# Linear attention beside a top-8 expert block: where ScalarE copies turned tile 2, which engine makes tile 3's root, and where G of tile 0 stands

## The chip, the core and the metric

One core of a Trainium2 chip. The metric is the device time of one execution in microseconds (us), the median of several runs. TensorE (PE) multiplies matrices, VectorE (DVE), ScalarE (ACT) and GpSimd (POOL) work on vectors, and SyncE (SP) issues most of the DMAs. Each engine runs its own instructions in order and waits for the others by semaphores. PSUM, where PE writes, has eight banks, called 0 to 7 here.

## What is computed

The input is x with 2048 rows of 640. Two blocks are added to it:

```python
xn = _layernorm(x)                        # over the 640 columns
# A: linear attention, 32 heads of 20
q, k, v = split(xn @ wqkv)
phi = lambda t: jnp.where(t > 0, t + 1, jnp.exp(t)) + 1e-6
pq, pk = phi(q), phi(k)
num = pq @ (pk.T @ v)                     # head by head
den = pq @ pk.sum(over rows) + 1e-6
A = (num / den) @ wo
# B: the 8 rows of xn with the largest xn @ w_r go through an expert
B = xn;  B[idx] += (silu(xs @ w_gate) * (xs @ w_up)) @ w_down * sigmoid(r[idx])
out = x + A + B
```

## The kernel before

The rows are cut into 16 tiles of 128 (t = 0 to 15), the columns into five pieces of 128 (`kc`). The order of every engine's instructions is the order in which the calls stand in the file: nothing is rescheduled, and an engine that waits holds back all that stands behind it.

A tile of the first phase passes these steps:

- `stat(t, b)` (L174): VectorE takes the statistics of one half of the row, and after the second half the mean and variance (`mv`).
- `root_act(t)` (L179) or `root_pool(t)` (L184): one over the standard deviation, `rs`. On ScalarE it is two one-column activations, Ln (L181) and Exp (L182); on GpSimd it is an addition (L186) and a power (L187).
- `norm_dve(t)` (L195): VectorE writes the normalised tile `xn` (L196).
- Turning the tile: tiles 0 to 3 by PE, later ones by DMA. `tr_pe(t)` (L212) is five transposes (L215) into banks 7 and 6. `tr_ev(t, V)` (L219) evicts them into `xnT`: ScalarE copies the first three pieces (L221), VectorE the other two (L226). The same two banks serve the next tile.
- `k_half(t, b)` (L233): five matmuls (L237) that give one half of k, 320 columns. Tile 1 uses banks 2 and 3, tile 2 banks 4 and 5, all others banks 0 and 1.
- `k_act(t, halves)` (L246): ScalarE evicts k. Each half takes two activations of 128 x 320, Exp into `ek` (L251) and Relu into `rk` (L252); after half 1 of all tiles but tile 0, a one-column copy takes the router's score (L254). `k_phi(t)` (L257) then makes phi on VectorE (L259).

`router_col` (L151) puts the router's weights into the k weights as one more column, by one transpose and a copy on ScalarE (L153); since tile 0's k comes before that, `router_0` (L155) gets its score by five one-column matmuls (L157), copied from bank 6 at L163.

Of q there are 20 units of 128 x 512. `q_mm(u, bank)` (L271) is five matmuls (L274), `q_act` (L280) two activations (L283, L284). Units 0 and 2 use bank 7, unit 1 bank 0. G is the product of xn and phi of k, summed over all tiles in banks 2 to 6: `g1(t)` (L264) is five matmuls of 512 columns (L266) per tile. Those banks are free for it once the k of tiles 1 and 2 and the router's score of tile 0 have been read.

The order of calls around the change is written out by hand in L389 to L465 of the file. The middle of it:

```python
    root_act(2)
    router_col()
    k_act(0)
    ...
    root_pool(3)
    const_sel8()
    k_half(1, 0)
    tr_pe(2)
    k_half(1, 1)
    tr_ev(2, V)
    router_0()
    k_act(1)
```

Behind it follow `k_half(2, 0)`, `tr_pe(3)`, `k_half(2, 1)`, `tr_ev(3, V)`, `k_act(2)`, both halves of tile 3, `q_mm(0)`, `q_mm(1, 0)`, `g1(0)`, `q_mm(2)` and tile 4 on PE.

Of the kernel before, what the change touches and what calls it, by code (L numbers as in the profile page):

```python
# [8 lines left out]
P = 128  # L9
# [9 lines left out]
HW = 320  # L19
# [10 lines left out]
BF16 = mybir.dt.bfloat16  # L30
# [8 lines left out]
def kernel(  # L39
# [22 lines left out]
    evk = ctx.enter_context(tc.tile_pool(name="evk", bufs=4))  # L62
# [34 lines left out]
    def load_x(a, b):  # L97
        SP.dma_start(x_sb[:, a:b, :], x_v[:, a:b, :])
# [52 lines left out]
    def router_col():  # L151
        PE.transpose(psb[:, 6, 512 : 512 + KC], wr5[:], ident[0:KC, 0:KC])
        A.copy(wk[:, :, D], psb[:, 6, 512 : 512 + KC])  # L153

    def router_0():  # L155
        for kc in range(KC):
            PE.matmul(  # L157
                ps[:, 6, 400:401], lhsT=xnT[:, kc, 0:P], rhs=wk[:, kc, D : D + 1],
                start=(kc == 0), stop=(kc == KC - 1),
            )  # L160
# [13 lines left out]
    def stat(t, b):  # L174
        V.bn_stats(out=stats[:, t, b, :], in_=x_sb[:, t, b * HW : (b + 1) * HW])  # L175
        if b:
            V.bn_aggr(out=mv[:, t, :], in_=stats[:, t, :, :])  # L177

    def root_act(t):  # L179
        sl = slice(t, t + 1)  # L180
        A.activation(lg[:, sl], mv[:, t, 1:2], AF.Ln, bias=eps5[:])  # L181
        A.activation(rs[:, sl], lg[:, sl], AF.Exp, scale=-0.5)  # L182

    def root_pool(t, n=1):  # L184
        sl = slice(t, t + n)
        G.tensor_scalar_add(t2[:, sl], mv[:, sl, 1], EPS_BF16)  # L186
        G.tensor_tensor(out=rs[:, sl], in0=t2[:, sl], in1=mhalf[:, 0:n], op=ALU.pow)  # L187
# [31 lines left out]
    def tr_ev(t, other=A):  # L219
        dst = xnT[:, :, t * P : (t + 1) * P]  # L220
        A.copy(dst[:, 0:3, :], psb[:, 7, 0 : 3 * P].rearrange("p (k f) -> p k f", k=3))  # L221
        src = psb[:, 6, 0 : 2 * P].rearrange("p (k f) -> p k f", k=2)
        if other is A:
            A.copy(dst[:, 3:, :], src)
        else:
            V.tensor_copy(dst[:, 3:, :], src)  # L226

    def tr_dma(t):
        nc.sync.dma_start_transpose(xnT[:, :, t * P : (t + 1) * P], xn[:, t, :])
# [3 lines left out]
    def k_half(t, b):  # L233
        b0 = K_BANK.get(t, 0)
        n = HW + (b if t else 0)
        for kc in range(KC):
            PE.matmul(  # L237
                ps[:, b0 + b, 0:n],
                lhsT=xnT[:, kc, t * P : (t + 1) * P],
                rhs=wk[:, kc, b * HW : b * HW + n],  # L240
                start=(kc == 0), stop=(kc == KC - 1),
            )

    kev = {}

    def k_act(t, halves=(0, 1)):  # L246
        b0 = K_BANK.get(t, 0)
        e = evk.tile([P, 2, HW], BF16, tag="ek", name=f"ek{t}")
        r = evk.tile([P, 2, HW], BF16, tag="rk", name=f"rk{t}")
        for b in halves:  # L250
            A.activation(e[:, b, :], ps[:, b0 + b, 0:HW], AF.Exp)  # L251
            A.activation(r[:, b, :], ps[:, b0 + b, 0:HW], AF.Relu)  # L252
            if b and t:
                A.copy(r_all[:, t : t + 1], ps[:, b0 + 1, HW : HW + 1])  # L254
        kev[t] = e, r

    def k_phi(t):  # L257
        e, r = kev.pop(t)
# [5 lines left out]
    def g1(t):  # L264
        for c in range(5):
            PE.matmul(  # L266
                ps[:, 2 + c, :], lhsT=xn[:, t, c * P : (c + 1) * P], rhs=pk[:, t, 0:512],
                start=(t == 0), stop=(t == T - 1),
            )

    def q_mm(u, bank=7):  # L271
        tb, m = u // KC, u % KC
        for kc in range(KC):
            PE.matmul(  # L274
                ps[:, bank, :], lhsT=wq[:, kc, m * P : (m + 1) * P],
                rhs=xnT[:, kc, tb * 512 : (tb + 1) * 512],
                start=(kc == 0), stop=(kc == KC - 1),
            )

    def q_act(u, bank=7):  # L280
        e = evq.tile([P, 512], BF16, tag="eq", name=f"eq{u}")
        r = evq.tile([P, 512], BF16, tag="rq", name=f"rq{u}")
        A.activation(e[:], ps[:, bank, :], AF.Exp)  # L283
        A.activation(r[:], ps[:, bank, :], AF.Relu)  # L284
        kev["q", u] = e, r
# [76 lines left out]
    def const_sel8():  # L362
        cst["sel8"] = sb("sel8", [P, C], F32)
        G.memset(cst["sel8"][:], 0.0)
        for j in range(4):
            G.affine_select(
                out=cst["sel8"][:], in_=cst["sel8"][:], compare_op=ALU.not_equal, fill=1.0,
                base=-32 * j, pattern=[[-1, C]], channel_multiplier=1,
            )
# [9 lines left out]
    def stats2(t):  # L379
        stat(t, 0)  # L380
        stat(t, 1)
# [22 lines left out]
    tr_ev(1, V)  # L404
    root_act(2)
    router_col()
    k_act(0)
    stat(3, 0)
    norm_dve(2)
    stat(3, 1)  # L410
    root_pool(3)
    const_sel8()
    k_half(1, 0)
    tr_pe(2)
    k_half(1, 1)
    tr_ev(2, V)
    router_0()
    k_act(1)
    stat(4, 0)
    norm_dve(3)  # L420
# [4 lines left out]
    k_half(2, 1)  # L425
    tr_ev(3, V)
    k_act(2)
    stat(5, 0)
    k_phi(0)
# [11 lines left out]
    norm_dve(5)  # L441
    tr_dma(5)
    q_act(0)
    q_mm(1, 0)
    q_act(1, 0)
    k_phi(1)
    norm_dve(6)
    tr_dma(6)
    load_x(10, 16)
    g1(0)  # L450
    stats2(7)
    root_pool(7)
    k_phi(2)
# [472 lines left out]
```

## Time and profile before

| what | us |
|---|---|
| median of 3 runs | 112.06 |
| lowest and highest | 111.9, 112.12 |
| the profiled execution | 111.9 |
| its span, first to last instruction | 110.2 |
| PE busy in the span | 105.5 |
| DVE busy | 83.9 |
| ACT busy | 61.4 |
| POOL busy | 41.3 |

The profiled execution is the one with the lowest time; 1.7 us of it lie outside the span. In a row of the order of time, the first number is the start in us from the span's start, the second the length of the row; x15 means fifteen instructions in one row, and a bracket gives the idle time ahead of it and what ended it. An instruction on ScalarE or VectorE can be issued while the one before it still runs, so rows overlap. The end of a matmul lies some way behind the issue of the next one.

### The profile page before, as it was taken

To read this page: it belongs to the slowest core of one execution; us is meant where nothing else is said; L and a number is where in the kernel's file an instruction comes from. 1 tells how busy PE (TensorE), PEld (TensorE's weight loads), DVE (VectorE), ACT (ScalarE), POOL (GpSimd) and SP (SyncE) were. 2 spreads that over 40 slices of the span, in tenths; PEclk is the share of its full clock that TensorE was granted. 3 is DMA by queue.
4 is the path that set the end of the run, shared out by engine and by line. 5 is a ranking of instruction groups with operands and counts; after the bars stand their busy time and mean duration, and the time that the engine had idled before them with its cause. 6 is when DMAs were issued, how large, how long until landed. Compare 5 with 4: busy or idle time off the path is not lost.

```text
span 110.2 us, 2558 instructions
## 1 busy us (share of the span) xinstructions
PE 105.5 (96%) x926; PEld 61.9 (56%) x926; DVE 83.9 (76%) x186; ACT 61.4 (56%) x158; POOL 41.3 (38%) x89
## 2 busy tenths in 40 slices
PE   5999999999999999999999999999999999999990
PEld 2256645565555555555437879444447766666660
DVE  1798998799999998756739844698599665788880
ACT  1549996797967666655048372588985645000000
POOL 6913564202366648899997330000000410000310
DMA  2999334792678799889999979549939295783333
GB/s 71 333 343 332 112 68 91 177 273 59 182 184 180 175 125 254 188 169 352 230 301 381 363 245 286 156 110 314 348 60 171 20 343 189 194 320 101 110 122 119
DMA packets 28551, 22.46 MB, mean 204 GB/s; under 512 B 11634, under 2 KB 27258, under 8 KB 28538
## 3 DMA queue, kind: packets, MB, share of 16 engines
q1 hardware_dynamic: 23664, 18.44, 62.3%
q10 hardware_dynamic: 4810, 3.85, 11.4%
q8 instruction: 7, 0.11, 0.5%
q14 instruction: 6, 0.05, 0.2%
q0 software_dynamic: 64, 0.01, 0.2%
HBM read 14.79 MB, written 5.43 MB: 183 GB/s over the span
## 4 chain that ended last, share of the span: by engine, by line
PE 89%; ACT 3%; DMA 2%; DVE 2%; issue 1%; ACTq 0%
PE ps L274 20%; PE ps L823 19%; PE ps L237 18%; PE ps L266 16%; PE ps L522 4%; DMA x_sb<-in_A_x_dram 2%; PE ps L658 2%; PE ps L675 2%; PE ps L758 2%; PE ps L849 1%; PE ps L215 1%; PE ps L590 1%; PE ps L687 1%; DVE xn L196 1%; PE ps L768 1%; DVE stats L175 1%
## 5 line engine op out<-in xcount | busy, mean ns | idle before, releaser
L237 PE MATMUL ps<-wk,xnT 128*128 128x320 bf16 (+1 forms) x160 | 24.8, 300 | 0.1
L274 PE MATMUL ps<-xnT,wq 128*128 128x512 bf16 x100 | 23.7, 379 | 0.0
L823 PE MATMUL ps<-late,pqT 128*128 128x320 bf16 x150 | 21.8, 300 | 0.1
L237 PEld LDWEIGHTS <-xnT 128*128 128x128 bf16 x160 | 15.1, 97 | 8.6 <-ACT xnT L221 0.9
L266 PE MATMUL ps<-pk,xn 128*128 128x512 bf16 x80 | 19.6, 379 | 0.0
L251 ACT ACTIVATE ek<-ps 128x320 bf16<-128x320 f32 x32 | 14.8, 461 | 8.1 <-PE ps L237 8.1
L823 PEld LDWEIGHTS <-pqT 128*128 128x128 bf16 x150 | 13.9, 98 | 7.2 <-DVE pqT L631 1.9
L283 ACT ACTIVATE eq<-ps 128x512 bf16<-128x512 f32 x20 | 12.0, 598 | 8.9 <-PE ps L274 8.9
L290 DVE SCALAR_TENSOR_TENSOR pqT<-eq,rq 128x512 bf16<-128x512 bf16 x20 | 14.2, 709 | 3.5 <-ACT rq L284 3.4
L832 DVE TENSOR_TENSOR o<-ps,x_sb 128x640 bf16<-128x640 f32 x15 | 12.3, 823 | 5.4 <-PE ps L823 3.0
L175 DVE BATCH_NORM_STATS2 stats<-x_sb 128x6 f32<-128x320 bf16 x32 | 14.7, 473 | 2.1 <-DMA x_sb<-in_A_x_dram 1.9
L259 DVE SCALAR_TENSOR_TENSOR pk<-ek,rk 128x640 bf16<-128x640 bf16 x16 | 14.0, 874 | 2.4 <-ACT rk L252 2.3
L274 PEld LDWEIGHTS <-wq 128*128 128x128 bf16 x100 | 9.4, 98 | 10.6 <-issue 0.7
L252 ACT ACTIVATE rk<-ps 128x320 bf16<-128x320 f32 x32 | 14.7, 460 | 0.0
L207 POOL TENSOR_SCALAR x_sb<-x_sb,rs,nm 128x640 bf16<-128x640 bf16 x13 | 12.6, 982 | 0.6
L266 PEld LDWEIGHTS <-xn 128*128 128x128 bf16 x80 | 7.6, 98 | 8.1
L284 ACT ACTIVATE rq<-ps 128x512 bf16<-128x512 f32 x20 | 11.9, 593 | 0.0
L186 POOL TENSOR_SCALAR t<-mv 128x1 bf16<-128x1 f32 x12 | 3.8, 318 | 20.3 <-DVE mv L177 20.0
L196 DVE TENSOR_SCALAR xn<-x_sb,mv,rs 128x640 bf16<-128x640 bf16 x16 | 8.2, 515 | 3.3 <-POOL rs L187 2.8
L187 POOL TENSOR_TENSOR rs<-t,mhalf 128x1 f32<-128x1 bf16 x12 | 10.1, 839 | 1.0
L874 POOL DMA_INDIRECT s_dram<-y,idx_i x1 | 1.6, 1595 | 20.9 <-ACT y L870 20.9
L859 ACT CAST o<-ps 128x160 bf16<-128x160 f32 x1 | 0.3, 293 | 13.9 <-PE ps L849 13.9
(128 smaller groups left out, 105.5 us busy)
## 6 DMA issues: line engine op xcount, KB each, us to landing
wg<-in_B_w_gate_dram SPq DMA_DIRECT2D x5, 384.0 KB, 3.4
wu<-in_B_w_up_dram SPq DMA_DIRECT2D x5, 384.0 KB, 9.0
wd<-in_B_w_down_dram SPq DMA_DIRECT2D x4, 480.0 KB, 11.2
spare<-rd SPq DMA_DIRECT2D x3, 640.0 KB, 5.3
rd<-rden ACTq DMA_DIRECT2D x1, 1280.0 KB, 7.3
out_dram<-o SPq DMA_DIRECT2D x8, 160.0 KB, 1.9
out_dram<-o ACTq DMA_DIRECT2D x7, 160.0 KB, 2.8
wo<-in_A_wo_dram SPq DMA_DIRECT2D x2, 500.0 KB, 7.0
```

Of the source, the lines that this page charges most:

```text
L175: V.bn_stats(out=stats[:, t, b, :], in_=x_sb[:, t, b * HW : (b + 1) * HW])
L207: G.tensor_scalar(out=x_sb[:, t, :], in0=x_sb[:, t, :], scalar1=rs1[:, sl], scalar2=nm[:, sl], op0=ALU.mult, op1=ALU.add,)
L237: PE.matmul(ps[:, b0 + b, 0:n], lhsT=xnT[:, kc, t * P : (t + 1) * P], rhs=wk[:, kc, b * HW : b * HW + n], start=(kc == 0), stop=(kc == KC ...
L251: A.activation(e[:, b, :], ps[:, b0 + b, 0:HW], AF.Exp)
L252: A.activation(r[:, b, :], ps[:, b0 + b, 0:HW], AF.Relu)
L259: V.scalar_tensor_tensor(out=pk[:, t, :].rearrange("p (b f) -> p b f", b=2), in0=e[:], scalar=1.0, in1=r[:], op0=ALU.min, op1=ALU.add,)
L266: PE.matmul(ps[:, 2 + c, :], lhsT=xn[:, t, c * P : (c + 1) * P], rhs=pk[:, t, 0:512], start=(t == 0), stop=(t == T - 1),)
L274: PE.matmul(ps[:, bank, :], lhsT=wq[:, kc, m * P : (m + 1) * P], rhs=xnT[:, kc, tb * 512 : (tb + 1) * 512], start=(kc == 0), stop=(kc == K ...
L283: A.activation(e[:], ps[:, bank, :], AF.Exp)
L290: V.scalar_tensor_tensor(out=pqT[:, m, tb * 512 : (tb + 1) * 512], in0=e[:], scalar=1.0, in1=r[:], op0=ALU.min, op1=ALU.add,)
L823: PE.matmul(ps[:, b0 + b, 0:HW], lhsT=pqT[:, kc, t * P : (t + 1) * P], rhs=Ms[:, kc, b * HW : (b + 1) * HW], start=(kc == 0), stop=(kc == ...
L832: V.tensor_tensor(out=o_t[:], in0=ps[:, b0 : b0 + 2, 0:HW], in1=x_sb[:, t, :].rearrange("p (b f) -> p b f", b=2), op=ALU.add,)
```

## The change

Three things change, and nothing is computed differently:

- `k_act(0)` is cut in two. Half 0 of tile 0's k is evicted where all of it was; half 1 comes behind `tr_ev(2, V)`. So ScalarE's copy of turned tile 2 stands between the halves. For this `k_act` now makes its two tiles at the first call and keeps them for the second.
- The root of tile 3 is made by `root_act(3)` on ScalarE, behind that copy and ahead of half 1, where it was `root_pool(3)` on GpSimd.
- `g1(0)` stands ahead of `q_mm(1, 0)`; it stood four calls behind `q_act(1, 0)`.

```diff
     def k_act(t, halves=(0, 1)):
         b0 = K_BANK.get(t, 0)
-        e = evk.tile([P, 2, HW], BF16, tag="ek", name=f"ek{t}")
-        r = evk.tile([P, 2, HW], BF16, tag="rk", name=f"rk{t}")
+        if t not in kev:
+            e = evk.tile([P, 2, HW], BF16, tag="ek", name=f"ek{t}")
+            r = evk.tile([P, 2, HW], BF16, tag="rk", name=f"rk{t}")
+            kev[t] = e, r
+        e, r = kev[t]
         for b in halves:
             A.activation(e[:, b, :], ps[:, b0 + b, 0:HW], AF.Exp)
             A.activation(r[:, b, :], ps[:, b0 + b, 0:HW], AF.Relu)
             if b and t:
                 A.copy(r_all[:, t : t + 1], ps[:, b0 + 1, HW : HW + 1])
-        kev[t] = e, r
...
     root_act(2)
     router_col()
-    k_act(0)
+    k_act(0, (0,))
     stat(3, 0)
     norm_dve(2)
     stat(3, 1)
-    root_pool(3)
     const_sel8()
     k_half(1, 0)
     tr_pe(2)
     k_half(1, 1)
     tr_ev(2, V)
+    root_act(3)
+    k_act(0, (1,))
     router_0()
     k_act(1)
...
     q_act(0)
+    g1(0)
     q_mm(1, 0)
     q_act(1, 0)
     k_phi(1)
     norm_dve(6)
     tr_dma(6)
     load_x(10, 16)
-    g1(0)
```

ScalarE in the first phase, from the second activation of tile 0's half 0 to the copy of turned tile 3. `ek0` and `rk0` are tile 0's, `ek1` and `rk1` tile 1's; the first `xnT` row is the copy of turned tile 2, the last that of tile 3. Before:

```order
L252 ACTIVATE rk0_212<-ps_72 128x320
L251 ACTIVATE ek0_211<-ps_72 128x320
L252 ACTIVATE rk0_212<-ps_72 128x320
L221 COPY xnT_80<-ps_72 128x3x128
L251 ACTIVATE ek1_259<-ps_72 128x320
L252 ACTIVATE rk1_260<-ps_72 128x320
L251 ACTIVATE ek1_259<-ps_72 128x320
L252 ACTIVATE rk1_260<-ps_72 128x320
L254 CAST r_all_129<-ps_72 128x1
L221 COPY xnT_80<-ps_72 128x3x128
```

The same stretch of ScalarE in the changed kernel, where L254, L255 and L257 are what L251, L252 and L254 were:

```order
L255 ACTIVATE rk0_212<-ps_72 128x320
L221 COPY xnT_80<-ps_72 128x3x128
L181 ACTIVATE lg_125<-mv_123,eps5_106 128x1
L182 ACTIVATE rs_126<-lg_125 128x1
L254 ACTIVATE ek0_211<-ps_72 128x320
L255 ACTIVATE rk0_212<-ps_72 128x320
L254 ACTIVATE ek1_259<-ps_72 128x320
L255 ACTIVATE rk1_260<-ps_72 128x320
L254 ACTIVATE ek1_259<-ps_72 128x320
L255 ACTIVATE rk1_260<-ps_72 128x320
L257 CAST r_all_129<-ps_72 128x1
L221 COPY xnT_80<-ps_72 128x3x128
```

The copy of turned tile 2 has moved up past two activations, and two new one-column activations and those two now stand between it and tile 1's k. Nine instructions stand between the two copies where five stood.

PE at the first q units (`wq`) and G of tile 0 (`pk`, `xn`), with what each row waits for; rows that only repeat are left out. Before, the rows are the last matmul of unit 0, the first of unit 1, the first of G and the first of unit 2:

```order
L274 LDWEIGHTS wq_84
L274 MATMUL ps_72<-xnT_80,wq_84 128x512
L274 MATMUL ps_72<-xnT_80,wq_84 128x512 [waits Activation_49]
...
L266 LDWEIGHTS xn_79
L266 MATMUL ps_72<-pk_82,xn_79 128x512 [waits DVE_49]
...
L274 MATMUL ps_72<-xnT_80,wq_84 128x512 [waits Activation_49]
```

And in the changed kernel, the last matmul of unit 0, the first of G, its third, the first of unit 1 and the first of unit 2 (L276 and L268 are what L274 and L266 were):

```order
L276 MATMUL ps_72<-xnT_80,wq_84 128x512
L268 LDWEIGHTS xn_79
L268 MATMUL ps_72<-pk_82,xn_79 128x512 [waits DVE_49]
...
L268 MATMUL ps_72<-pk_82,xn_79 128x512 [waits Activation_49]
...
L276 LDWEIGHTS wq_84
L276 MATMUL ps_72<-xnT_80,wq_84 128x512 [waits Activation_49]
...
L276 MATMUL ps_72<-xnT_80,wq_84 128x512 [waits Activation_49]
```

G's five matmuls and unit 1's five have changed places; G now waits for ScalarE itself, which it did not where unit 1's wait stood ahead of it. VectorE and SyncE keep their order; GpSimd loses the two instructions of tile 3's root.

## Prediction

> **What bounds the kernel now.** I read the page's totals first, then the chain of work that ended last, then busy time by stretches, then the order of time on each engine around the change. The page's first line gives busy time per engine; the next line below is the chain by engine; the two group lines show count, busy time, mean ns of one and, last, the idle time in front of the group.
>
> ```profile
> PE 105.5 (96%) x926; PEld 61.9 (56%) x926; DVE 83.9 (76%) x186; ACT 61.4 (56%) x158; POOL 41.3 (38%) x89
> ...
> PE 89%; ACT 3%; DMA 2%; DVE 2%; issue 1%; ACTq 0%
> ...
> L237 PE MATMUL ps<-wk,xnT 128*128 128x320 bf16 (+1 forms) x160 | 24.8, 300 | 0.1
> L274 PE MATMUL ps<-xnT,wq 128*128 128x512 bf16 x100 | 23.7, 379 | 0.0
> ```
>
> Over the whole run TensorE is the bound: 89% of the chain, and its two largest groups have 0.1 and 0.0 us of idle time in front of them. ScalarE has 3% of the chain, so I ask where. The busy time by stretches (length; busy us of PE, PE's weight loads, DVE, ACT, POOL; granted clock; DMA) answers:
>
> ```profile
> 8.84:12.52 3.68, 3.58 (x35) 2.38 (x34) 3.21 (x10) 3.68 (x14) 1.89 (x8) 1.00 0.78 273
> 12.52:16.30 3.78, 3.78 (x24) 2.09 (x23) 3.70 (x10) 3.78 (x14) 2.04 (x5) 1.00 0.27 60
> ```
>
> From 8.84 to 16.30 ScalarE is never idle: 3.68 of 3.68 us, then 3.78 of 3.78. It is the engine without room exactly where the change adds work to it. The chain in order of time (start, length) goes through it there:
>
> ```profile
> 10.33 0.38 ACT xnT L221
> 10.71 0.05 issue
> 10.76 0.85 PE ps L237 x5
> ...
> 12.00 2.07 PE ps L237 x15
> ```
>
> and the waits of PE's weight loads from 10 to 20 us (total, times, longest) name the same pair twice:
>
> ```profile
> PEld L237 <- ACT xnT L221: 0.4, 2, 0.2
> ```
>
> Those two waits are for ScalarE's copies of turned tile 2 and turned tile 3. From the second on PE runs without a break:
>
> ```profile
> 7.56 0.45 PE L215 MATMUL ps<-ident,xn 128*128 128x128 bf16 x5
> ...
> 9.43 0.44 PE L215 MATMUL ps<-ident,xn 128*128 128x128 bf16 x5
> ...
> 10.39 0.27 PE L157 MATMUL ps<-wk,xnT 128*128 128x1 bf16 x5
> 10.76 0.85 PE L237 MATMUL ps<-wk,xnT 128*128 128x320 bf16 x5
> 11.55 0.45 PE L215 MATMUL ps<-ident,xn 128*128 128x128 bf16 x5
> 11.84 2.23 PE L237 MATMUL ps<-wk,xnT 128*128 128x321 bf16 x15
> 13.91 2.32 PE L274 MATMUL ps<-xnT,wq 128*128 128x512 bf16 x10
> 16.06 1.24 PE L266 MATMUL ps<-pk,xn 128*128 128x512 bf16 x5
> 17.14 1.24 PE L274 MATMUL ps<-xnT,wq 128*128 128x512 bf16 x5
> 18.22 1.53 PE L237 MATMUL ps<-wk,xnT 128*128 128x321 bf16 x10
> ```
>
> The row at 11.84 holds three halves of k: the second of tile 2 and both of tile 3, fifteen matmuls that issue over 13.91 - 11.84 = 2.07 us, 0.138 each. Tile 3's first therefore issues at about 11.84 + 5 x 0.138 = 12.53. The ScalarE rows (start, length) show how close that is:
>
> ```profile
> 7.94 0.48 ACT L221 COPY xnT<-ps 128x384 bf16<-128x384 bf16 x1 [0.92 <-PE ps L215]
> 8.32 0.30 ACT L181 ACTIVATE lg<-mv,eps 128x1 f32<-128x1 f32 x1
> 8.65 0.20 ACT L182 ACTIVATE rs<-lg 128x1 f32<-128x1 f32 x1
> 8.84 0.18 ACT L153 COPY wk<-ps 128x5 bf16<-128x5 bf16 x1
> ...
> 9.55 0.46 ACT L251 ACTIVATE ek<-ps 128x320 bf16<-128x320 f32 x1
> ...
> 10.18 0.52 ACT L221 COPY xnT<-ps 128x384 bf16<-128x384 bf16 x1
> 10.54 0.51 ACT L251 ACTIVATE ek<-ps 128x320 bf16<-128x320 f32 x1
> ...
> 11.93 0.55 ACT L221 COPY xnT<-ps 128x384 bf16<-128x384 bf16 x1
> ...
> 14.00 0.59 ACT L252 ACTIVATE rk<-ps 128x320 bf16<-128x320 f32 x1
> ...
> 16.76 0.59 ACT L284 ACTIVATE rq<-ps 128x512 bf16<-128x512 f32 x1
> ...
> 23.25 0.20 ACT L182 ACTIVATE rs<-lg 128x1 f32<-128x1 f32 x1
> 23.36 0.58 ACT L283 ACTIVATE eq<-ps 128x512 bf16<-128x512 f32 x1
> ```
>
> The copy of turned tile 3 ends at 11.93 + 0.55 = 12.48, 0.05 before PE needs it. It has no slack: what delays it delays PE, and PE then never pauses long enough to make it up.
>
> **The change, part by part.** *The early copy of turned tile 2.* For tile 1 the copy began 7.94 - 7.56 = 0.38 us after the first transpose. Tile 2's transposes start at 9.43, which is PE's own order and does not move, so the copy can start at 9.81 instead of 10.18. ScalarE would have come free at 9.55, where the row of the third activation of tile 0 stood; it now idles 0.26 us.
>
> *The root of tile 3.* In the one earlier place with the same sequence Ln starts 8.32 - 7.94 = 0.38 after the copy, Exp 0.33 after Ln, and ends 0.20 later: Ln 10.19, Exp 10.52, end 10.72. Its input must be there, and the norm behind it must be free; these are the rows of VectorE and GpSimd:
>
> ```profile
> 9.77 0.21 DVE L177 BATCH_NORM_AGGREGATE mv<-stats 128x2 f32<-128x12 f32 x1
> ...
> 11.02 0.47 DVE L196 TENSOR_SCALAR xn<-x_sb,mv,rs 128x640 bf16<-128x640 bf16 x1 [0.35 <-POOL rs L187]
> ...
> 12.65 0.81 DVE L259 SCALAR_TENSOR_TENSOR pk<-ek,rk 128x640 bf16<-128x640 bf16 x1
> ...
> 10.40 0.58 POOL L187 TENSOR_TENSOR rs<-t,mhalf 128x1 f32<-128x1 bf16 x1
> ```
>
> The variance is ready at 9.98, and VectorE waited 0.35 for the root, so the norm of tile 3 moves from 11.02 to about 10.75. What GpSimd loses (its root ended at 10.98) costs nothing and only lets the constants behind it start sooner.
>
> *What PE gains first.* With the copy of tile 2 done at about 10.3, k of tile 2 waits for nothing but the five one-column matmuls at 10.39, so it may start at about 10.65 instead of 10.76. Tile 3's transposes follow 5 x 0.138 = 0.69 later at 11.34 (the norm ends at 11.22, no longer late), 0.21 sooner than 11.55. The second half of tile 2 then starts at 11.63 and has issued by 12.32.
>
> *What is late next: the copy of turned tile 3.* Between Exp's issue and this copy ScalarE must now run half 1 of tile 0, which took 10.18 - 9.55 = 0.63, and all of tile 1, which took 11.93 - 10.54 = 1.39. The issue behind Exp follows 0.11 later (23.25 to 23.36) or 0.19 (8.65 to 8.84; that one also waited for PE). So the copy starts at 10.52 + 0.11 + 0.63 + 1.39 = 12.65, **0.72 us later** than 11.93. The same 0.72 comes out as a sum of what is new ahead of it: idle 0.26, Ln 0.33, Exp 0.11, and 0.02 because Ln follows a copy after 0.38 where an activation did after 0.36. It lasts 0.48 (first row) to 0.55, since the queue behind a pause is shorter, so it ends between 13.13 and 13.20; with the 0.19 at 13.28. I take 13.17, against 12.48: **+0.69 us**, with +0.65 and +0.80 as ends. PE idles from 12.32 to about 13.2, and the 0.21 won before is lost inside that pause.
>
> *What stands behind it on ScalarE.* The evictions of tiles 2 and 3 and of q unit 0 shift by the same 0.69, as does PE's work that feeds them; both keep their distance. Tile 0's phi on VectorE started at 12.65 and needs half 1, now done near 11.4: hidden.
>
> *G of tile 0 ahead of q unit 1.* Ten matmuls change places, and none is added. Shifted by 0.69, q unit 0 runs from 14.60 to 15.68 and G starts at 15.68. It needs tile 2's banks and the router bank, which tile 2's evictions and the small copies release before tile 3's evictions start (the second of those, at 14.00, shifts to 14.69), and tile 0's phi, done at 12.65 + 0.81 = 13.46. No wait. Unit 1 moves to 16.75 and needs bank 0, free at 14.69 plus at most 0.59 = 15.28. Its own eviction now runs at about 18.0, and the half of tile 4 that reuses bank 0 starts at 18.22 + 0.69 + 5 x 0.138 = 19.60; the eviction's second activation ends near 18.0 + 0.5 + 0.59 = 19.1. Hidden with 0.5 us to spare; without that cover the excess would go straight onto PE. Since q and G had 0.0 idle, there was nothing to gain either: I take 0, between 0 and +0.1.
>
> *Sum.* The profiled execution took 111.9 us, of which 110.2 is the span; + 0.69 gives a span of 110.9 and a time of 112.6. The median of the three runs is 112.06, 0.16 above that execution, so the forecast is 112.06 + 0.69 = **112.75**.
>
> **Rivals.** *The earlier norm decides, not the copy.* If ScalarE could still copy turned tile 3 by 12.3, the 0.21 won at the transposes would stay: 112.06 - 0.21 = 111.85. That point needs the nine instructions from Exp's issue at 10.52 to the copy's end inside 1.8 us; the rows say 0.11 + 0.63 + 1.39 + 0.5 = 2.63. For it speaks only that activations could be slowed by something that the new order relieves; against it, ScalarE's 100% busy stretch at even steps. Chance 0.07, and a little more for a larger gain from a cause that I don't see, 0.04.
>
> *The pause is made up later.* Then the time stays near 112.06. It would need a later PE wait for something that doesn't shift. Tile 4's turned input by DMA is the only near one, and PE met it at 18.22 with no gap (17.14 + 1.08). Chance 0.02.
>
> *The clock falls after the pause.* PE's first nine matmuls and its later k matmuls stand in these rows:
>
> ```profile
> 1.24 4.02 PE L146 MATMUL ps<-zw 128*128 128x512 bf16 x9 [1.24 <-DVE zw L134]
> 5.58 0.71 PE L215 MATMUL ps<-ident,xn 128*128 128x128 bf16 x5 [0.32 <-DVE xn L196]
> ...
> 6.65 0.85 PE L237 MATMUL ps<-wk,xnT 128*128 128x320 bf16 x5
> ```
>
> Nine in 4.02 us is about 0.43 each, twice the 2.15 / 10 = 0.215 of the q matmuls of the same size at 13.91, though the granted clock reads 1.00 throughout: PE starts at half rate and is at full rate by 6.65, after a gap of 0.32 at 5.26. If a pause of 0.9 brought half rate back for another 4 us, 2 us would be lost: 112.75 + 2.0 = 114.75. No row shows a pause of that length. Chance 0.03.
>
> The Trainium skill ("TensorE: Matmul & The Clock Gate", Part 1) says that the clock halves only after an idle window of about 3.4 us, which leaves 112.75; its section on psum-queue depth-cycling speaks against the change, saying that short idles between groups can bring the low rate back, which is this rival. The full rate at 6.65 after the 0.32 gap fits the first; no row here decides for 0.9.
>
> **How the numbers follow.** Forecast 0.84, clock 0.03, earlier norm 0.07, larger gain 0.04, made up 0.02. The copy's ends give 112.71 to 112.86; the runs of before spread from -0.16 to +0.06 about their median, and a start of G or unit 1 that is slightly late adds up to 0.1. That makes 112.5 to 113.0; I widen it to 112.4 to 113.1 for what the pause may do to the steps of both engines. By 0.2%, about what a measurement of this kernel can tell from no change (0.22 us), the cases give: slower 0.87, same 0.09 (the earlier norm's 0.21 falls just inside, with the made-up case), faster 0.04.
>
> **What would show it.** Right: ScalarE idle about 0.26 us ahead of tile 2's copy near 9.8; tile 3's transposes near 11.3; its copy starting near 12.65; PE's weight loads waiting once for that copy, with PE idle some 0.9 us until 13.2; then the same steps as before, 0.69 later, and a span of 110.9. Wrong: tile 3's copy before 12.3, PE without a gap at 12.3, a second gap ahead of tile 4's half in bank 0, or matmuls at twice their step after 13.2.

## The result, and the profile after

| | before | changed |
|---|---|---|
| median, us | 112.06 (6 runs) | 112.72 (6 runs) |
| lowest to highest | 111.88 to 112.12 | 112.37 to 112.99 |
| the profiled execution | 111.9 | 112.37 |
| its span | 110.2 | 110.6 |
| ratio to before | | 1.0063, 95% interval 1.0047 to 1.0078 |

The changed kernel is slower by 0.66 us in the medians; 112.75 was forecast. Ratios, here and below, leave out single runs that lie more than 1.5% above the fastest of their kernel, and the medians keep them. The lines of the page that answer to those of before, the chain by engine and the two groups (count, busy us, mean ns, idle time ahead of the group and what ended most of it):

```profile
PE 105.1 (95%) x926; PEld 61.7 (56%) x926; DVE 83.2 (75%) x186; ACT 61.9 (56%) x160; POOL 40.3 (36%) x87
...
PE 89%; ACT 4%; DMA 2%; DVE 2%; issue 0%; ACTq 0%
...
L237 PE MATMUL ps<-wk,xnT 128*128 128x320 bf16 (+1 forms) x160 | 25.0, 300 | 1.0 <-ACT xnT L221 1.0
L276 PE MATMUL ps<-xnT,wq 128*128 128x512 bf16 x100 | 23.8, 379 | 0.0
```

The k group's idle time has gone from 0.1 to 1.0 us, and all of it is put down to ScalarE's copies of turned tiles (L221): 0.78 is the pause shown below, and 0.24 stands at 6.48, ahead of the change, in this profile and not in that of before. ScalarE's share of the chain has gone from 3 to 4%. The waits of PE itself, from 8 to 60 us (total, times, longest), hold one line, where before there was none:

```profile
PE ps L237 <- ACT xnT L221: 0.8, 1, 0.8
```

ScalarE around the change, in order of time:

```profile
9.05 0.44 ACT L255 ACTIVATE rk<-ps 128x320 bf16<-128x320 f32 x1
9.62 0.48 ACT L221 COPY xnT<-ps 128x384 bf16<-128x384 bf16 x1
9.99 0.30 ACT L181 ACTIVATE lg<-mv,eps 128x1 f32<-128x1 f32 x1
10.32 0.20 ACT L182 ACTIVATE rs<-lg 128x1 f32<-128x1 f32 x1
10.43 0.42 ACT L254 ACTIVATE ek<-ps 128x320 bf16<-128x320 f32 x1
...
11.07 0.44 ACT L254 ACTIVATE ek<-ps 128x320 bf16<-128x320 f32 x1
...
12.34 0.21 ACT L257 CAST r_all<-ps 128x1 bf16<-128x1 f32 x1
12.38 0.55 ACT L221 COPY xnT<-ps 128x384 bf16<-128x384 bf16 x1
```

With the 0.18 us added that is explained below, the first copy, Ln and Exp stand within 0.02 us of the forecast, and the second copy starts 0.09 sooner than forecast; it ends at 12.93. PE:

```profile
9.25 0.44 PE L215 MATMUL ps<-ident,xn 128*128 128x128 bf16 x5
9.53 0.85 PE L237 MATMUL ps<-wk,xnT 128*128 128x321 bf16 x5
10.22 0.26 PE L157 MATMUL ps<-wk,xnT 128*128 128x1 bf16 x5
10.34 0.84 PE L237 MATMUL ps<-wk,xnT 128*128 128x320 bf16 x5
11.06 0.45 PE L215 MATMUL ps<-ident,xn 128*128 128x128 bf16 x5
11.35 0.85 PE L237 MATMUL ps<-wk,xnT 128*128 128x321 bf16 x5
12.98 1.54 PE L237 MATMUL ps<-wk,xnT 128*128 128x320 bf16 x10 [0.78 <-ACT xnT L221]
14.36 1.24 PE L276 MATMUL ps<-xnT,wq 128*128 128x512 bf16 x5
15.43 1.24 PE L268 MATMUL ps<-pk,xn 128*128 128x512 bf16 x5
16.51 2.32 PE L276 MATMUL ps<-xnT,wq 128*128 128x512 bf16 x10
18.67 1.53 PE L237 MATMUL ps<-wk,xnT 128*128 128x321 bf16 x10
```

The fifteen matmuls that were one row have become five, a pause of 0.78 us (the bracket), and ten. Behind it the steps are those of before.

To compare executions, one shift has to be taken out: in this one tile 2's transposes stand 0.18 us earlier than in the profile of before (9.25 against 9.43). The change does not do that. In the fourteen profiles of this case the time of this first transpose falls in two groups, 9.25 to 9.27 and 9.41 to 9.44, and the changed kernel has been met in both (9.41 in e11). In the first group PE's first five transposes, near 5.57, take 0.45 us, in the second 0.71: the half rate that PE starts with has ended ahead of them in the one and not in the other. So I measure from tile 2's first transpose to the first matmul of tile 4's k: 18.22 - 9.43 = **8.79** us before and 18.67 - 9.25 = **9.42** now, 0.63 more. This distance spans all that the change moves, and is used for every run below. Each comes from one profiled execution.

### The profile page after: what moved, and what is told of

The parts are those of the page before. It is cut to its first block, busy times and chain, and to the rows that moved or that the text cites. A ratio compares the mean times of both kernels' runs of the same rounds, so it can differ in the third digit from the quotient of the medians.

```text
span 110.6 us, 2558 instructions
## 1 busy us (share of the span) xinstructions
PE 105.1 (95%) x926; PEld 61.7 (56%) x926; DVE 83.2 (75%) x186; ACT 61.9 (56%) x160; POOL 40.3 (36%) x87
## 4 chain that ended last, share of the span: by engine, by line
PE 89%; ACT 4%; DMA 2%; DVE 2%; issue 0%; ACTq 0%
PE ps L276 20%; PE ps L826 19%; PE ps L237 18%; PE ps L268 16%; PE ps L525 4%; DMA x_sb<-in_A_x_dram 2%; PE ps L661 2%; PE ps L678 2%; PE ps L761 2%; PE ps L852 1%; ACT xnT L221 1%; PE ps L593 1%; PE ps L690 1%; ACT ek L254 1%; ACT rk L255 1%; PE ps L215 1%
## 5 line engine op out<-in xcount | busy, mean ns | idle before, releaser
L276 PE MATMUL ps<-xnT,wq 128*128 128x512 bf16 x100 | 23.8, 379 | 0.0
L268 PE MATMUL ps<-pk,xn 128*128 128x512 bf16 x80 | 19.6, 379 | 0.0
L254 ACT ACTIVATE ek<-ps 128x320 bf16<-128x320 f32 x32 | 14.6, 457 | 8.1 <-PE ps L237 8.1
L292 DVE SCALAR_TENSOR_TENSOR pqT<-eq,rq 128x512 bf16<-128x512 bf16 x20 | 13.7, 685 | 3.4 <-ACT rq L286 3.4
L276 PEld LDWEIGHTS <-wq 128*128 128x128 bf16 x100 | 9.4, 98 | 10.6 <-issue 0.7
L255 ACT ACTIVATE rk<-ps 128x320 bf16<-128x320 f32 x32 | 14.6, 456 | 0.0
L268 PEld LDWEIGHTS <-xn 128*128 128x128 bf16 x80 | 7.6, 98 | 8.1
L187 POOL TENSOR_TENSOR rs<-t,mhalf 128x1 f32<-128x1 bf16 x11 | 9.4, 858 | 0.9
```

The source lines that it names most:

```text
L268: PE.matmul(ps[:, 2 + c, :], lhsT=xn[:, t, c * P : (c + 1) * P], rhs=pk[:, t, 0:512], start=(t == 0), stop=(t == T - 1),)
L276: PE.matmul(ps[:, bank, :], lhsT=wq[:, kc, m * P : (m + 1) * P], rhs=xnT[:, kc, tb * 512 : (tb + 1) * 512], start=(kc == 0), stop=(kc == K ...
L292: V.scalar_tensor_tensor(out=pqT[:, m, tb * 512 : (tb + 1) * 512], in0=e[:], scalar=1.0, in1=r[:], op0=ALU.min, op1=ALU.add,)
```

## The experiments

Theory: ScalarE's queue ahead of the copy of turned tile 3 sets when PE goes on, and the pause goes through to the end. Rivals: the cost sits in one part alone (early copy, root, G's place); added work on ScalarE costs wherever it stands; a short delay is made up later.

| run | distance, us | against 8.79 | median, us | ratio to before, 95% interval |
|---|---|---|---|---|
| the change | 9.42 | +0.63 | 112.72 | 1.0047 to 1.0078 |
| e11, the change again | 9.42 | +0.63 | 112.52 | 1.0032 to 1.0073 |
| e1, G's place alone | 8.79 | 0.00 | 111.91 | 0.9987 to 1.0012 |
| e2, ScalarE's part alone | 9.42 | +0.63 | 112.54 | 1.0028 to 1.0056 |
| e3, early copy alone | 9.02 | +0.23 | 112.26 | 0.9991 to 1.0040 |
| e4, root alone | 9.18 | +0.39 | 112.31 | 1.0007 to 1.0036 |
| e5, tile 3's copy earlier | 8.70 | -0.09 | 112.0 | 0.9995 to 1.0057 |
| e6, the same, G back | 9.08 | +0.29 | 112.31 | 1.0021 to 1.0071 |
| e7, before + 1 activation | 9.14 | +0.35 | 112.48 | 1.0031 to 1.0075 |
| e10, the change + 1 | 9.76 | +0.97 | 112.88 | 1.0063 to 1.0113 |
| e8, the change + 3 | 12.45 | +3.66 | 114.66 | 1.0150 to 1.0257 |
| e9, tile 3's copy first | 8.67 | -0.12 | 111.9 | 0.9965 to 1.0014 |
| e12, e9 + x loaded sooner | 8.68 | -0.11 | 113.99 | 1.0137 to 1.0210 |

The kernel before took 111.97, 111.84, 112.04 and 112.0 beside e1 to e4, e5 to e8, e9 to e11 and e12.

**e1: G's place alone.**

```diff
# before.py
     q_act(0)
+    g1(0)
     q_mm(1, 0)
...
-    g1(0)
```

> The kernel before with G of tile 0 ahead of q unit 1 and nothing else. Theory (ScalarE's queue ahead of the copy of turned tile 3 sets when PE goes on; G's place is neutral): 112.06, within 0.1, PE without a gap between 12 and 20 us. Rival (G's new place carries part of the cost, by a wait for a bank): 112.3 or more, with a gap ahead of G, of unit 1 or of tile 4's half in bank 0.

The distance is the same to the hundredth, and the ratio is 1.0000. G's place is neutral in the kernel before. Together with e2 the rival that it carries part of the cost falls.

**e2: ScalarE's part alone.**

```diff
# after.py
     q_act(0)
-    g1(0)
     q_mm(1, 0)
...
     load_x(10, 16)
+    g1(0)
```

> The changed kernel with G of tile 0 put back behind q unit 1. Theory: as the changed kernel, 112.7 within 0.1, since bank 0 is released 0.4 us before unit 1 needs it. Rival (G's place carries part of the cost): nearer to 112.06; second rival (G's place hides a cost): above 112.9 with a wait ahead of unit 1.

112.54, with the change's distance of 9.42 and its pause of 0.78. All of the cost is in what ScalarE was given.

**e3 and e4: the two things that ScalarE was given, one at a time.**

```diff
# e3: before.py, the early copy alone
-    k_act(0)
+    k_act(0, (0,))
...
     tr_ev(2, V)
+    k_act(0, (1,))
# e4: before.py, the root alone
-    root_pool(3)
...
     tr_ev(2, V)
+    root_act(3)
```

> The kernel before with only the copy of turned tile 2 between the halves; tile 3's root on GpSimd and G where they were. Theory: of the 0.72 us only the idle 0.26 is left ahead of tile 3's copy, so about +0.2: 112.25, within 0.1. Rival (the root on ScalarE is the whole cost): 112.06. Rival (the early copy is the whole cost): 112.7.

> The kernel before with only tile 3's root moved to ScalarE, behind the copy of turned tile 2, which stays behind both halves of tile 0. Theory: Ln 0.33 and Exp 0.11 stand ahead of tile 3's copy, about +0.45: 112.5, within 0.1. Rival (the early copy is the whole cost): 112.06. Rival (the root is the whole cost): 112.7.

The early copy costs 0.23 us in the distance (the pause ahead of it was priced at 0.26), the root 0.39 (priced at 0.44), together 0.62 where the whole costs 0.63. The order of time on ScalarE has the root's step in e4:

```profile
10.20 0.52 ACT L221 COPY xnT<-ps 128x384 bf16<-128x384 bf16 x1
10.55 0.35 ACT L181 ACTIVATE lg<-mv,eps 128x1 f32<-128x1 f32 x1
10.93 0.20 ACT L182 ACTIVATE rs<-lg 128x1 f32<-128x1 f32 x1
11.04 0.42 ACT L251 ACTIVATE ek<-ps 128x320 bf16<-128x320 f32 x1
```

From Ln's issue to tile 1's first activation are 0.49 us, for two instructions that work on one column: Exp waits for Ln. Both rivals that put the cost on one part fall. In time e4 alone is clear of no change. Four of e3's twelve runs, 111.96 to 111.98, stand where the kernel before does, its interval takes in 1, and that it costs rests on its one trace.

**e7 and e10: a dose.** One more activation of 128 x 320 ahead of the copy of turned tile 3, of zeros into a part of phi of k that is overwritten later, in the kernel before (e7) and in the changed one (e10):

```diff
+    A.activation(pk[:, T - 1, 0:HW], zw[:, 0:HW], AF.Exp)
     tr_pe(3)
```

> The kernel before with one more 128 x 320 activation on ScalarE (of zeros, into a part of phi of k that is written later) between tile 1's eviction and the copy of turned tile 3. Theory: the copy has no slack, so all of its 0.32 us shows: 112.38, within 0.08. Rival (a short delay is made up later): 112.06 to 112.15.

> The changed kernel with one more activation of zeros ahead of the copy of turned tile 3. Theory: PE's pause grows from 0.78 to about 1.15 us and the time by 0.35, to about 113.0, at the full clock. Rival (the clock can fall after a pause of this length too, as it did in one half of the executions after 2.1 us): some executions 1 us or more above the others, with a granted clock below 1 behind the pause.

ScalarE in e7, from tile 1's one-column copy to the copy of turned tile 3:

```profile
11.64 0.28 ACT L254 CAST r_all<-ps 128x1 bf16<-128x1 f32 x1
11.68 0.59 ACT L425 ACTIVATE pk<-zw 128x320 bf16<-128x320 bf16 x1
12.05 0.59 ACT L221 COPY xnT<-ps 128x384 bf16<-128x384 bf16 x1
```

The added activation takes 0.37 us of the queue (11.68 to 12.05), and the distance grows by 0.35 in e7 and by 0.34 in e10: nearly all of the dose reaches PE, before the change and after it. The rival that a short delay is made up later falls; e7's time rose by 0.35 to 0.84 us by its interval, no less than the dose. In e10's profiled execution the pause was 1.13 us, and no run of e10 shows a mean granted clock below 0.996; two of its six, 113.13 and 113.5, lie above the rest, and their cause is not known.

**e8: three such activations in the changed kernel.**

> The changed kernel with three such activations at the same place. Theory: PE's pause grows by 0.96 us to about 1.6 and the time with it: 113.65, within 0.15, matmuls at the same steps behind it. Rival (a longer pause brings half rate back): 115 or more, with matmuls at twice their step.

A miss. The three took 1.44 us, 0.48 each and not 0.32 (12.37 to the copy's start at 13.81): the second and the third start at 12.93 and 13.43, only when the one before has ended. All three write one place, which may be why; no run tells that apart. That made the pause 2.12 us. And the runs fell in two groups: 113.69, 113.83 and 113.94, with a mean granted clock of 0.997 to 1.000, which the pause explains, and 115.37, 115.39 and 115.41, with 0.984 and 0.985. The median in the table, 114.66, lies between the groups and is the time of no run. The profiled execution is of the second group. Its busy time by stretches (after the busy columns: granted clock, DMA share, GB/s):

```profile
11.35:14.32 2.97, 0.85 (x8) 0.39 (x6) 2.90 (x10) 2.91 (x10) 1.06 (x3) 1.00 0.27 97
14.32:16.30 1.98, 1.79 (x10) 1.19 (x12) 1.79 (x5) 1.98 (x9) 1.74 (x3) 0.79 0.41 83
16.30:18.04 1.74, 1.70 (x4) 0.59 (x4) 1.38 (x5) 0.79 (x4) 0.29 (x1) 0.50 0.75 108
18.04:20.00 1.96, 1.96 (x9) 0.81 (x8) 1.19 (x4) 1.08 (x2) 1.25 (x2) 0.78 0.87 88
20.00:22.00 2.00, 2.00 (x12) 0.98 (x11) 1.97 (x6) 1.18 (x3) 0.00 (x0) 1.00 0.55 99
```

Behind the pause the granted clock falls to 0.50 and is back at 1.00 by 20. The prediction's clock rival can happen, then, but it was seen only with the longer pause: none of the changed kernel's twelve runs shows a mean clock below 0.997. The traces put no exact figure on the pause that it needs, and at one pause it came in three executions of six.

**e5 and e6: is it the work or the place?** The changed kernel with tile 1's eviction cut as well, so that the copy of turned tile 3 stands ahead of half 1 of it; e6 also puts G back behind unit 1.

```diff
# after.py
     router_0()
-    k_act(1)
+    k_act(1, (0,))
...
     tr_ev(3, V)
+    k_act(1, (1,))
     k_act(2)
```

> The changed kernel with tile 1's eviction cut too: half 0, then the copy of turned tile 3, then half 1 and the score. Theory: the copy of tile 3 starts near 11.9 and ends near 12.4, so PE goes on at about 12.45 instead of 12.53: 111.97, within 0.1, though ScalarE does as much as in the changed kernel. Rival (the work added to ScalarE costs wherever it stands, since ScalarE is full to 16.3): 112.5 or more.

> The kernel of the run before with G of tile 0 put back behind q unit 1. Theory: now unit 1 comes at about 14.9 and bank 0 is free only near 15.25, so PE waits about 0.35 us there: 112.3, within 0.1; G's place is neutral in the changed kernel only because its pause hides this wait. Rival (G's place never matters): 111.97.

PE in e5, from the second half of tile 2 on:

```profile
11.35 2.45 PE L237 MATMUL ps<-wk,xnT 128*128 128x321 bf16 x15
13.85 1.02 PE L276 MATMUL ps<-xnT,wq 128*128 128x512 bf16 x4
14.71 1.24 PE L268 MATMUL ps<-pk,xn 128*128 128x512 bf16 x5
```

ScalarE does the same work as in the changed kernel, the fifteen matmuls are one row again, and the distance is 0.09 below that of before: the rival that the added work costs wherever it stands falls for this place. That rests on the trace, of an execution of 111.81. The median, 112.0, agrees with the theory only by luck: seven of e5's twelve runs lie between 111.63 and 112.11 and five between 112.63 and 112.94, and the interval (-0.06 to +0.64 us) takes in both no change and the 0.57 that e2 costs. What makes those five longer was not traced. With G back the distance grows by 0.38, and PE waits ahead of unit 1 for bank 0:

```profile
13.85 1.03 PE L276 MATMUL ps<-xnT,wq 128*128 128x512 bf16 x4
15.10 1.24 PE L276 MATMUL ps<-xnT,wq 128*128 128x512 bf16 x5 [0.22 <-ACT rk L255]
```

Unit 1 starts 15.10 - 14.71 = 0.39 later than what stands there in e5, G; the bracket's 0.22 counts from the end of the row ahead. So G's place is neutral in the change only because the pause gives ScalarE time to free bank 0. Once the pause is gone, G ahead of unit 1 is worth 0.38 us of distance; the times of e5 and e6 have intervals that overlap.

**e9: the copy of turned tile 3 behind the first activation of tile 1.** For this `k_act` takes a third argument, which says whether it issues Exp, Relu or both.

```diff
# after.py
-    k_act(1)
+    k_act(1, (0,), "e")
...
     tr_ev(3, V)
+    k_act(1, (0,), "r")
+    k_act(1, (1,))
```

> The changed kernel with the copy of turned tile 3 behind only the first activation of tile 1, where tile 3's transposes are just done; the other three activations of tile 1 follow. Theory: PE has no gap at all ahead of tile 3 and goes on 0.2 us earlier than in the kernel with half of tile 1 ahead of the copy; against the kernel before 0.2 to 0.3 us less, 111.75 within 0.15, if ScalarE's backlog does not show further on, where unit 2 needs bank 7 at about the time that unit 0's eviction ends. Rival (ScalarE, full to 16.3, is the bound, and PE only waits later): 111.95 or more, with a gap ahead of unit 2.

Half of each. PE in the profiled execution:

```profile
9.41 0.44 PE L215 MATMUL ps<-ident,xn 128*128 128x128 bf16 x5
...
11.51 2.21 PE L237 MATMUL ps<-wk,xnT 128*128 128x321 bf16 x15
13.78 1.03 PE L279 MATMUL ps<-xnT,wq 128*128 128x512 bf16 x4
14.64 1.24 PE L271 MATMUL ps<-pk,xn 128*128 128x512 bf16 x5
15.72 2.53 PE L279 MATMUL ps<-xnT,wq 128*128 128x512 bf16 x10
18.08 1.53 PE L237 MATMUL ps<-wk,xnT 128*128 128x321 bf16 x10
...
50.26 1.54 PE L237 MATMUL ps<-wk,xnT 128*128 128x320 bf16 x10 [0.60 <-DMA xnT<-xn]
```

Tile 3 follows without a gap, at about 11.51 + 0.69 = 12.20, which is 2.79 after tile 2's first transpose where it was 3.10 before: the 0.31 are there. Then units 1 and 2 take 2.53 instead of 2.32, and the chain of work shows why, unit 0's eviction:

```profile
16.46 0.50 ACT rq L289
...
17.00 1.24 PE ps L279 x5
```

Unit 2 waits 0.21 for bank 7: ScalarE's backlog shows, as the rival had it, and 0.12 are left at tile 4. And tile 15's k waits 0.60 for its turned input. Of the twelve runs eight lie between 111.58 and 111.97 and four between 112.50 and 112.77; the profiled one is of the four. Its VectorE shows where tile 15 became late:

```profile
23.94 0.21 DVE L177 BATCH_NORM_AGGREGATE mv<-stats 128x2 f32<-128x12 f32 x1
25.35 0.49 DVE L175 BATCH_NORM_STATS2 stats<-x_sb 128x6 f32<-128x320 bf16 x1 [1.21 <-DMA x_sb<-in_A_x_dram]
```

VectorE waits 1.21 us for the load of x tiles 10 to 15, which was issued at 19.41 where it was at 18.92 before. So these statistics start 0.76 later than the 24.59 of before, and the norms stay late by as much: tile 15's starts at 46.29, where it did at 45.55 before. The clock is not it: all twelve runs show 0.996 or more. A second bound thus lies just behind the first: VectorE's chain and the turning by DMA. Whether the other three long runs have the same wait was not traced. Over all runs e9 is not clear of the kernel before (0.9965 to 1.0014).

**e12: e9 with that load issued sooner.**

```diff
# e9
     tr_dma(5)
+    load_x(10, 16)
     q_act(0)
...
     tr_dma(6)
-    load_x(10, 16)
```

> The kernel of e9 with the load of x tiles 10 to 15 issued ahead of the turning of tile 6 instead of behind it. Theory on what is left in e9 (that load lands at 24.8 to 25.3, VectorE waits 0.8 to 1.2 us for it, its chain to tile 15's turned input comes late, and PE waits there by 0.6 us in the profiled execution): the load is issued about 1.5 us sooner, VectorE's wait and PE's wait for tile 15 go, and nearly all executions take 111.5 to 111.8 (e9: 111.58 to 112.77). Rival (the load only contends with the turned tiles 5 and 6): no better than e9, 111.9 or more, with PE waiting for a turned tile near 21 to 24 us.

The rival was right, and by far: 113.99. VectorE's wait is gone (the same statistics start at 23.93, and tile 15's norm at 44.96, so that norm does follow the load), but PE's longest wait is now one for a turned tile, tile 6's:

```profile
21.76 1.24 PE L279 MATMUL ps<-xnT,wq 128*128 128x512 bf16 x5
24.46 1.54 PE L237 MATMUL ps<-wk,xnT 128*128 128x320 bf16 x10 [1.46 <-DMA xnT<-xn]
```

The chain of this execution holds 6.43 us of DMA from the issue of tile 6's turning at 17.98, against 2.6 to 4.3 us from issue to landing, median 2.7, for the turnings of before in that stretch. The distance at tile 4, 8.68, is that of e9, so the loss comes behind it. One of the six runs, 115.72, shows a mean granted clock of 0.984, as e8's long ones do; the traced one waited 1.46 us at full clock. No version tried here beats the kernel before beyond its interval.

**e11: the changed kernel again.**

> The changed kernel once more, beside the two others on one chip: 112.6, within 0.15. It tells whether the spread of its first six runs, 112.37 to 112.99, belongs to the kernel (some executions near 112.9 at the same pause) or to those runs.

112.52; the pause is 0.78 and the distance 9.42 once more. Five of six runs lie between 112.35 and 112.53, one at 113.02. The two traced executions, 112.37 and 112.53, have one and the same pause; the longer ones were not traced, and what makes single runs longer by half a microsecond stays open.

## Why the prediction was right, step by step

All from tile 2's first transpose, to take out the 0.18:

- **The early copy** was to start after 0.38; it did after 9.62 - 9.25 = 0.37.
- **The root**: Ln was to follow after 0.38, Exp after 0.33, the next activation after 0.11; measured 0.37, 0.33 and 0.11. The first two came from one earlier place with the same sequence, the 0.11 from a later one.
- **Half 1 of tile 0**: 0.63 forecast, 11.07 - 10.43 = 0.64 measured.
- **Tile 1's eviction**: 1.39 forecast, 12.38 - 11.07 = 1.31 measured. This is the term that was mis-sized. It was read off the kernel before as 11.93 - 10.54, as if ScalarE's queue alone had set the 11.93. There the one-column copy and the copy of turned tile 3 stood so:

```profile
11.82 0.27 ACT L254 CAST r_all<-ps 128x1 bf16<-128x1 f32 x1
11.93 0.55 ACT L221 COPY xnT<-ps 128x384 bf16<-128x384 bf16 x1
```

The second follows the first by 0.11; in the change, e3, e4 and e7, whatever follows this one-column copy follows by 0.04. And 11.93 is 0.38 after tile 3's first transpose (11.55), as the copy of turned tile 1, which did wait for its transposes, was 0.38 after its own. So 0.07 of the 1.39 was a wait for PE, which does not show as idle time because the row ahead had not ended. In the change that wait is gone: what is new ahead of the copy is 0.25 idle (9.62 - 9.05, less a step of 0.32), Ln 0.33, Exp 0.11 and 0.01 of step, less 0.07, which makes the 0.63 that was measured.

- **The copy of turned tile 3** started 3.13 after the first transpose against 2.50 before: +0.63, forecast +0.72. It lasted 0.55 as before, where the forecast had taken 0.52, so its end moved by 0.63 too, forecast +0.69, and PE's start as well. Between the copy's end and PE there was no slack, as the prediction had it; e7 showed that apart. Ahead of the copy's start there was the 0.07: e7's 0.37 moved that start by 0.30 and e10's by 0.36; in e7 the copy also lasted 0.04 longer.
- **What PE gained first** was larger than forecast: tile 3's transposes came 1.81 after tile 2's, where it was 2.12; -0.31, not -0.21. The five one-column matmuls issue within 0.12 us (10.22 to 10.34); I had waited for the end of their row. It bought nothing in the change, since the pause swallows it, as the forecast said; e9 shows it as 0.31.
- **The pause**: 0.9 forecast from issue to issue; 12.98 - (11.35 + 0.69) = 0.94 measured so, since the transposes came sooner still (the bracket's 0.78 counts from the end of the row ahead). What passes on is the copy's delay: the distance at tile 4 is up by the 0.63 of the copy. The forecast of 0.69 for the time lies near the medians' 0.66. That this is nearer than the distance's 0.63 is luck: beside e11 the same two kernels' medians differ by 0.48.
- **G ahead of unit 1**: 0 forecast, 0.00 in e1; e2 has the change's distance without it. Unit 1's eviction started at 17.79 and had ended by 18.9, ahead of the half that needs bank 0 at 18.67 + 0.69 = 19.36, so the forecast 0.5 of cover was there.

Of the rivals, the earlier norm happened and decided nothing. The made-up pause is refuted by e7. The clock did not fall in the change; e8 shows that it can.

## What to carry to other kernels

On a full engine that feeds the bound, look for the next instruction that the bound waits for, and count what the edit puts ahead of that one, idle time included; here one copy moved up by 0.38 us and two one-column activations pushed the next copy back by 0.63, while in e5's trace the same instructions cost nothing, with that copy ahead of half of the tile that it had waited behind. Take the length of a stretch of such a queue only after asking what set its end: here 0.07 of it was a wait that the busy share did not show. When a wait is taken away, ask which later instruction the same engine now serves late, and whether a swap elsewhere (G ahead of unit 1) is worth anything only once that is mended. And a move that gains 0.3 us locally may meet the next bound just behind: here bank 7, then the load of x that VectorE waits for.

## What the runs showed of the hardware

- **The clock after a pause.** After a PE pause of 2.12 us the profiled execution of e8 shows a granted clock of 0.50 from about 15.5 us, 1.2 after PE went on, to about 18.9, and three of six executions of that kernel were longer by 1.6 us. None of the twenty-four executions of the change, e11, e2 and e10, whose traced pauses are 0.78 and 1.13 us, has a mean clock below 0.996. The Trainium skill ("TensorE: Matmul & The Clock Gate", Part 1) gives about 3.4 us of idling as the condition; here less was enough, in some executions and not in others.
- **A load ahead of a turning by DMA.** With 960 KB issued just ahead of it, in e12, the turning of tile 6 took 6.43 us; the turnings of before in that stretch took 2.6 to 4.3, median 2.7.
- **A wait without idle time.** On ScalarE an instruction is issued while the row ahead still runs (steps of 0.32 us, rows of 0.44 and more), so the 0.07 us that the copy of turned tile 3 waited for its transposes in the kernel before stands inside a stretch that reads as 3.68 busy of 3.68.
